# Talking-heads attention with a gated feed-forward layer: the score jobs run one slot further ahead

## The chip, the cores and the metric

The kernel runs on one core of a Trainium2 chip. The metric is the time of one execution on the device, in microseconds. The core has five engines that run in parallel, each through its own instructions in order: TensorE (PE in the profile; PEld is its weight load), VectorE (DVE), ScalarE (ACT), GpSimd (POOL) and SyncE (SP), which here issues nearly all DMA transfers. Engines wait for each other by semaphores. TensorE writes its results to PSUM, in banks that this program names; the other engines read them there.

## What is computed

```python
# q, k, v: 4 batches, 12 heads, 448 rows, head size 64
scores = q @ k.T / 8                                     # 448x448 for each head
scores = einsum('bhij,hg->bgij', scores, w_pre)          # mixes the 12 heads ("pre-mix")
e      = exp(scores - rowmax(scores))
attn   = e / (rowsum(e) + 1e-9)
attn   = einsum('bhij,hg->bgij', attn, w_post)           # mixes them again ("post-mix")
x      = attn @ v                                        # heads side by side: 1792 x 768
out    = (sigmoid(x @ w_gate) * (x @ w_val)) @ w_out     # 768 -> 1536 -> 768
```

## The kernel before

The program has two stages. Attention comes first and takes somewhat less than half of the span; the gated layer follows, and some of its preparations (weights turned into small pieces) run between the steps of attention.

**Blocks and units.** The 448 queries of a batch are cut into blocks of 120, 120, 120 and 88 queries, and a block into units of 20 queries, in each of which all 12 heads are held. A block has 6, 6, 6 or 5 units, a batch 23, all four 92. `first` holds the first unit of each block: 0, 6, 12, 18, 23, 29, 35, 41, 46, 52, 58, 64, 69 and so on. So unit 38 lies in the third block of batch 1, and unit 61 in the third block of batch 2.

**Score jobs.** For each block there are six jobs of `scores` (L155), one for each pair of heads, numbered c. A job is eight matmuls into two PSUM banks, and then two copies from them into `st` in SBUF (`keep`, L163): the even head's by ScalarE, the odd one's by VectorE. The banks are mostly the one pair `qk`, so the next job's matmuls wait until both copies of the last are done. In the fill, before the first unit, some jobs use the banks of other steps (`pm`, `mx`), which are free by then.

**A unit's way.** `regroup` (L199) is two DMA transfers, issued on SP, from `st` into one of four buffers `T`, in which the heads lie along the partitions. Then `premix` (L209, eight matmuls), `rowmax` into `nm` (VectorE), `expo` into `e` (two ScalarE instructions), norm and scale into `ph` (mostly GpSimd), `p_lo` into `pl` (VectorE), `postmix` (48 small matmuls into `mx`) and `mix` (ScalarE, out of PSUM). Once a whole block is mixed, `av` multiplies by V: six steps, two in every second slot of the block after, each pair evicted to `xt` by ScalarE and stored.

**Slots.** The order on every engine is written by hand, one slot for each unit and six ahead of the first (numbers -6 to -1, the fill). Slot s issues, in this order: on SP the regroup of unit s+6 (`LEAD` = 6) and the stores that are due; norm and scale of unit s+1; pre-mix and row maxima of unit s+3; the matmuls of the first score job planned for s; the first half of the exponentials of unit s+3, and after it the two copies of that job; `p_lo` of s+1; post-mix and mix of s; the second half of the exponentials; then what else is planned for the slot (loads of `k`, `q` and `v` on SP, the sums `v_abs` on ScalarE); then `av` and `moe.early`, the gated layer's preparations (loads into `raws` and a ScalarE step of line 1104); and last, if one is planned, a second score job. Each engine takes its own instructions in this order, and nothing but semaphores keeps the engines in the same slot.

**Where the score jobs stand.** `at(slot, function, ...)` plans a call, and `spread` divides a count evenly over slots. Before, the six jobs of block bi are spread from slot `first[bi-1] - 6` to slot `first[bi] - 6`, so the last of them stands one slot ahead of the block's first regroup. Where the block before has six units, that is a job in each slot. Where it has five, six jobs fall on five slots, and the first of these takes two. The `q` load of a block is planned four slots ahead of its first job. The six `k` loads of the next batch are spread over some slots in the middle of a batch, in the rest of the slot, behind its regroup. The first block's jobs run ahead of all slots (`ahead`).

Of the kernel before, what the change touches and what calls it, by code (L numbers as in the profile page):

```python
# [41 lines left out]
def _attention(ctx, tc, ins, B, H, S, D, xs, raws, make_moe):  # L42
# [4 lines left out]
    NP = H // 2  # L47
# [30 lines left out]
    def two_banks(pool, tag):  # L78
        return pool.tile([128, 2, 512], F32, tag=tag, name=tag)

    def qk_banks():
        return [ps_qk.tile([128, 512], F32, tag="qk", name="qk") for _ in range(2)]
# [47 lines left out]
    PB = NBK // B  # L130
    first = [blk[3] for blk in blocks] + [NU]
# [23 lines left out]
    def scores(bi, c, sc):  # L155
        b, n = blocks[bi][0], R * blocks[bi][4]
        q, k = q_t[bi], k_t[b, c]
        for s0, s1 in ((0, 64), (64, max(n, 100))):
            for e in range(2):
                rows = slice(64 * e, 64 * e + 64)  # L160
                nc.tensor.matmul(sc[e][s0:s1, :S], lhsT=q[c][rows, s0:s1], rhs=k[rows, :], start=True, stop=True)  # L161

    def keep(bi, c, e, sc):  # L163
        n = R * blocks[bi][4]
        if c == e == 0:
            st_t[bi] = stg[bi % ST].tile([QB, H, S], F32, tag="st", name="st")
        (nc.vector.tensor_copy if e else nc.scalar.copy)(st_t[bi][:n, 2 * c + e], sc[e][:n, :S])  # L167
# [41 lines left out]
    def premix(u):  # L209
        T = t_bufs[u % len(t_bufs)]  # L210
        banks = units[u][2]
        for x in range(2):
            for i, bank in enumerate(banks):
                rows = slice(64, 64 + HK) if i else slice(0, 64)
                nc.tensor.matmul(pm[bank][64 * x:64 * x + 64, :S], lhsT=w1[rows], rhs=T[rows, x], start=True, stop=True)  # L215

    def rowmax(u):
        nm = sm.tile([128, 2], F32, tag="nm", name="nm")
        for i, bank in enumerate(units[u][2]):
            nc.vector.tensor_reduce(nm[:, i:i + 1], pm[bank][:, :S], axis=AX.X, op=ALU.max, negate=True)  # L220
        nm_t[u] = nm

    def expo(u, i):
        if i == 0:
            e_t[u] = ep.tile([128, 2, S], F32, tag="e", name="e")
            ss_t[u] = sm.tile([128, 2], F32, tag="ss", name="ss")
        nc.scalar.activation(out=e_t[u][:, i], in_=pm[units[u][2][i]][:, :S], func=AF.Exp, bias=nm_t[u][:, i:i + 1],  # L227
                             scale=1.0, accum_out=ss_t[u][:, i:i + 1])

    def norm(u):  # L230
        ss = ss_t[u][:, :len(units[u][1])]
        (nc.vector if u >= NU - LAST else nc.gpsimd).tensor_scalar(ss, ss, 1e-9, 1.0 / P_UP, op0=ALU.add, op1=ALU.mult)
        nc.vector.reciprocal(ss, ss)  # L233

    def scale(u):

        ph = pp.tile([128, 2, S], F16, tag="ph", name="ph")
        for i in range(len(units[u][1])):
            e, ss = e_t[u][:, i], ss_t[u][:, i:i + 1]
            if u >= NU - LAST:  # L240
                nc.scalar.activation(out=ph[:, i], in_=e, func=AF.Copy, scale=ss)  # L241
            else:
                nc.gpsimd.tensor_scalar(ph[:, i], e, ss, 1.0, op0=ALU.mult, op1=ALU.mult)  # L243
        p_t[u] = [ph]

    def p_lo(u):
        pl = pp.tile([128, 2, S], F16, tag="pl", name="pl")
        for i in range(len(units[u][1])):
            nc.vector.scalar_tensor_tensor(pl[:, i], e_t[u][:, i], ss_t[u][:, i:i + 1], p_t[u][0][:, i],  # L249
                                           op0=ALU.mult, op1=ALU.subtract)  # L250
        p_t[u].append(pl)
# [14 lines left out]
    def mix(u):  # L266
        bi, r0s = units[u][:2]
        out = mixes[bi % 2].rearrange("p j h s -> p (j h) s")[:, :, r0s[0]:r0s[-1] + R]
        nc.scalar.activation(out=out.rearrange("p g (y r) -> p y g r", r=HALF), in_=mx_t.pop(u), func=AF.Copy,  # L269
                             scale=1.0 / (P_UP * W_UP))  # L270
# [4 lines left out]
    def flush():  # L275
        while stores:
            nc.sync.dma_start(out=stores[0][0], in_=stores.pop(0)[1])
# [31 lines left out]
    LEAD = 6  # L309
# [5 lines left out]
    def at(slot, fn, *args):  # L315
        plan.setdefault(slot, []).append((fn, args))

    def spread(i, n, s0, s1):
        return s0 + i * (s1 - s0) // n

    taken = {EARLY_AT[k] + slot for k in range(moe.EARLY) for slot in (11, 12)}
    for b in range(B):
        f = first[PB * b]
        for u in range(NQ):
            at(f + 2 + 2 * u, v_load, b, u)
        s = f + 5
        for i in range(H // 2):
            s = max(s + 1, f + 6 + 2 * (2 * i // QUAD))
            while s in taken:
                s += 1  # L330
            at(s, v_sum, b, i)
        if b % 2:
            at(s + 1, v_bound, b, 0)
        if b == 1:
            for step, slot in enumerate(BOUND[1:]):
                at(s + 1 + slot, v_bound, b, step + 1)
        for c in range(NP if b else 0):
            at(spread(c, NP, first[PB * (b - 1)] + 6, first[PB * b - 1] - LEAD - 2), k_load, b, c)
    for bi in range(1, NBK):
        s0, s1 = first[bi - 1] - LEAD, first[bi] - LEAD  # L340
        for c in range(NP):
            at(spread(c, NP, s0, s1), scores, bi, c)
        if bi > 1:
            at(s0 - 4, q_load, bi)
    for bi in range(NBK):
        s0 = first[bi + 1]
        s1 = first[bi + 2] if bi + 2 < len(first) else s0
# [58 lines left out]
    def rows_until(u, done):  # L406
        while done < min(NU, u + 1):
            regroup(done)
            done += 1
        return done  # L410

    next_dma = 0
    for s in range(min(min(plan), -LEAD), max(plan) + 1):
        next_dma = rows_until(s + LEAD, next_dma)
        flush()
        todo = plan.get(s, ())
        jobs = [args for fn, args in todo if fn is scores]
        ahead_u = [(s + SOFT, i) for i in range(len(units[s + SOFT][1]))] if 0 <= s + SOFT < NU else []
        if 0 <= s + 1 < NU:
            norm(s + 1)  # L420
            scale(s + 1)
        if ahead_u:
            premix(s + SOFT)
            rowmax(s + SOFT)

        def gated():
            for i in range(len(units[s][1])):
                moe.slot(units[s][3] + i)

        soon = NU - 7 <= s < NU  # L430
        if soon:
            for c in hooks.pop(s, ()):
                c.close()
            gated()

        def job(bi, c):
            if s == -LEAD:
                sc = pm[2:]
            elif s in (-4, -2):
                mx = two_banks(ps_mx, "mx")  # L440
                sc = [mx[:, e] for e in range(2)]
            else:
                sc = qk_banks()
            scores(bi, c, sc)
            return lambda e: keep(bi, c, e, sc)

        kept = job(*jobs[0]) if jobs else None
        for i, e in enumerate(ahead_u[:1]):
            expo(*e)
        if kept:  # L450
            kept(0)
            kept(1)
        for c in hooks.get(s, ()):
            c.close()
        if 0 <= s + 1 < NU:
            p_lo(s + 1)
        tail = (av, moe.between, moe.early)
        if s == NU - 1:
            nc.scalar.activation(out=iw, in_=sw, func=AF.Sigmoid)
        if 0 <= s < NU:  # L460
            postmix(s)
        elif s >= NU:
            moe.slot(NG + s - NU)
        if 0 <= s < NU:
            mix(s)
        for e in ahead_u[1:]:
            expo(*e)
        while late:
            late.pop(0)()
        for fn, args in todo:  # L470
            if fn is not scores and fn not in tail:
                fn(*args)
        if s >= NU - LEAD - 3:
            next_dma = rows_until(s + 1 + LEAD, next_dma)
        if 0 <= s < NU and not soon:
            gated()
        for fn, args in todo:
            if fn in tail:
                fn(*args)
        for args in jobs[1:]:  # L480
            kept = job(*args)
            kept(0)
            kept(1)
    return moe
# [21 lines left out]
class _Moe:  # L506
# [14 lines left out]
    NP = 7  # L521
# [797 lines left out]
```

## Time and profile before

| | |
|---|---|
| time, median of three runs | 787.21 us (787.09 to 788.61) |
| the profiled execution's own time | 788.01 us |
| its span in the trace | 786.2 us |
| granted TensorE clock, mean | 0.995 |
| TensorE busy | 761.5 us, 97% |
| VectorE busy | 630.9 us, 80% |
| ScalarE busy | 572.9 us, 73% |
| GpSimd busy | 250.5 us, 32% |

The trace is from one execution, another than the three timed ones. Its time is 1.8 us longer than the span between its first and last instruction. Busy shares are means over two stages that differ: in attention VectorE and ScalarE have far more to do than in the gated layer.

### The profile page before, as it was taken

What the parts mean: (1) busy time and instruction counts of PE and PEld (TensorE: products, weight loads), DVE (VectorE), ACT (ScalarE), POOL (GpSimd) and SP (SyncE); (2) the same over time, 40 slices, a digit from 0 to 9 for tenths busy, and PEclk for the clock granted to TensorE, in tenths of its full rate; (3) what the DMA queues carried; (4) which work ended last, traced back from release to release, by engine and by line L of the source; (5) the groups of instructions that cost most, each with busy time, mean ns of one, the idle gap of its engine ahead of it and who ended that gap; (6) DMA issues with size and microseconds to landing.
All of it is one profiled execution on the core that took longest, in us unless ns stands there. A gap on an engine that the chain in (4) does not pass through costs nothing.

```text
span 786.2 us, 23669 instructions
## 1 busy us (share of the span) xinstructions
PE 761.5 (97%) x9623; PEld 422.2 (54%) x9623; DVE 630.9 (80%) x1093; ACT 572.9 (73%) x1145; POOL 250.5 (32%) x418
## 2 busy tenths in 40 slices
PE   8899999899999999879999999999999999999998
PEld 2365666566556666554555555555555555555554
DVE  4988899799978998879997989588876999997111
ACT  4899999889999899886876866577756784563000
POOL 2564547354544455200312222224222221010000
PEclk9999999999999999989999999999999999999999
DMA  6786668758886574738507284664567788995001
GB/s 198 242 272 222 209 219 261 259 172 245 253 262 199 188 240 167 234 84 293 176 3 257 83 304 151 250 222 141 198 208 264 272 307 311 387 347 212 36 36 70
DMA packets 81118, 166.17 MB, mean 211 GB/s; under 512 B 20721, under 2 KB 58193, under 8 KB 81009
## 3 DMA queue, kind: packets, MB, share of 16 engines
q1 hardware_dynamic: 73006, 133.14, 51.5%
q0 software_dynamic: 7728, 31.27, 10.3%
q8 instruction: 75, 1.23, 0.7%
q14 instruction: 35, 0.28, 0.1%
q10 hardware_dynamic: 274, 0.25, 0.1%
HBM read 87.77 MB, written 38.15 MB: 160 GB/s over the span
## 4 chain that ended last, share of the span: by engine, by line
PE 84%; ACT 7%; DMA 3%; DVE 2%; issue 1%; SPq 1%; POOL 1%; DVEq 0%; ACTq 0%; POOLq 0%
PE bank L1173 34%; PE bank L1184 18%; PE pm L215 9%; PE av L290 8%; PE qk L161 7%; PE mx L261 7%; DMA T<-st 2%; ACT e L227 2%; ACT mix L269 2%; ACT m L1152 1%; DVE nm L220 1%; ACT st L167 1%; DVE m L1157 1%; PE pm L161 1%; SPq L205 1%
## 5 line engine op out<-in xcount | busy, mean ns | idle before, releaser
L1173 PEld LDWEIGHTS <-m 128*128 128x128 f16 x1512 | 147.7, 98 | 140.1 <-DVE m L1157 2.1
L1173 PE MATMUL bank<-m,m 128*128 128x448 f16 x1116 | 214.2, 352 | 1.7 <-DVE m L1157 1.7
L243 POOL TENSOR_SCALAR ph<-e,ss 128x448 f16<-128x448 f32 x173 | 108.0, 635 | 139.7 <-DVE ss L233 90.6
L227 ACT ACTIVATE e<-pm,nm 128x448 f32<-128x448 f32 x177 | 113.8, 643 | 28.2 <-DVE nm L220 25.3
L220 DVE TENSOR_REDUCE nm<-pm 128x1 f32<-128x448 f32 x177 | 101.6, 613 | 31.1 <-PE pm L215 25.9
L249 DVE SCALAR_TENSOR_TENSOR pl<-e,ss,ph 128x448 f16<-128x448 f32 x180 | 114.7, 677 | 0.7 <-ACT ph L241 0.7
L215 PE MATMUL pm<-T,w 64*64 64x448 f32 (+1 forms) x708 | 105.2, 560 | 7.4 <-DMA T<-st 3.6
L1184 PEld LDWEIGHTS <-m 128*128 128x128 f16 x756 | 74.0, 98 | 69.0
L269 ACT ACTIVATE mix<-mx 128x960 f32<-128x960 f32 (+1 forms) x92 | 104.6, 1137 | 2.7 <-PE mx L261 2.7
L261 PEld LDWEIGHTS <-ph 64*128 64x128 f16 x2880 | 63.8, 94 | 70.9 <-issue 44.3
L161 PE MATMUL qk<-k,q 64*64 64x448 f32 (+1 forms) x712 | 96.2, 539 | 1.0 <-ACT st L167 1.0
L1184 PE MATMUL bank<-m,m 128*128 128x448 f16 x468 | 92.9, 352 | 0.0
L290 PE MATMUL av<-mix,v 128*64 128x120 f32 (+1 forms) x1472 | 82.9, 266 | 0.6 <-ACT xt L298 0.6
L261 PE MATMUL mx<-w2hi,ph 64*128 64x60 f16 x1440 | 71.4, 189 | 7.2 <-ACT mix L269 6.8
L1173 PE MATMUL bank<-m 128*128 128x448 f16 x396 | 77.9, 352 | 0.0
L290 PEld LDWEIGHTS av<-mix,v 128*64 128x64 f32 x1472 | 72.8, 139 | 3.9 <-ACT xt L298 1.0
L1110 POOL CAST raws<-raws 128x768 f16<-128x768 bf16 x28 | 30.9, 1102 | 137.8 <-ACT raws L1104 137.8
L261 PE MATMUL mx<-w2hi,pl 64*128 64x60 f16 x1440 | 70.5, 188 | 1.1 <-issue 0.5
L261 PE MATMUL mx<-w2lo,ph 64*128 64x60 f16 x1440 | 70.5, 188 | 0.0
L1104 ACT ACTIVATE raws<-raws 128x768 int16<-128x768 int8 (+1 forms) x72 | 60.4, 839 | 10.8 <-POOL raws L1110 10.5
L1200 DVE TENSOR_TENSOR m<-bank,m 128x448 f32<-128x448 f32 x72 | 44.5, 620 | 23.6 <-PE bank L1173 15.3
L261 PEld LDWEIGHTS <-pl 64*128 64x128 f16 x1440 | 61.3, 93 | 1.1 <-DVE pl L249 1.1
(136 smaller groups left out, 1081.9 us busy)
## 6 DMA issues: line engine op xcount, KB each, us to landing
T<-st SPq DMA_DIRECT2D x175, 210.0 KB
m<-w SPq DMA_DIRECT2D x60, 384.0 KB
raws<-in_w_dram SPq DMA_DIRECT2D x28, 767.6 KB
hs<-m POOLq DMA_DIRECT2D x48, 224.0 KB, 3.4
m<-hs SPq DMA_DIRECT2D x15, 672.0 KB
w<-m POOLq DMA_DIRECT2D x21, 384.0 KB, 4.4
w<-raws POOLq DMA_DIRECT2D x20, 384.0 KB, 4.6
v<-in_vb_dram SPq DMA_DIRECT2D x12, 512.0 KB
```

The source lines that it names most:

```text
L161: nc.tensor.matmul(sc[e][s0:s1, :S], lhsT=q[c][rows, s0:s1], rhs=k[rows, :], start=True, stop=True)
L215: nc.tensor.matmul(pm[bank][64 * x:64 * x + 64, :S], lhsT=w1[rows], rhs=T[rows, x], start=True, stop=True)
L220: nc.vector.tensor_reduce(nm[:, i:i + 1], pm[bank][:, :S], axis=AX.X, op=ALU.max, negate=True)
L227: nc.scalar.activation(out=e_t[u][:, i], in_=pm[units[u][2][i]][:, :S], func=AF.Exp, bias=nm_t[u][:, i:i + 1], scale=1.0, accum_out=ss_t[u ...
L243: nc.gpsimd.tensor_scalar(ph[:, i], e, ss, 1.0, op0=ALU.mult, op1=ALU.mult)
L249: nc.vector.scalar_tensor_tensor(pl[:, i], e_t[u][:, i], ss_t[u][:, i:i + 1], p_t[u][0][:, i], op0=ALU.mult, op1=ALU.subtract)
L261: nc.tensor.matmul(mx[:, x, i, jb * HK:(jb + 1) * HK], lhsT=p[rows, i, JB[jb]:JB[jb] + 128], rhs=w[rows], start=(k == 0), stop=(k == 2))
L269: nc.scalar.activation(out=out.rearrange("p g (y r) -> p y g r", r=HALF), in_=mx_t.pop(u), func=AF.Copy, scale=1.0 / (P_UP * W_UP))
L290: nc.tensor.matmul(av_t[bi][64 * i:64 * i + 64, c % 2, :n], lhsT=vt[b, u][:, h + i, jb, :], rhs=mixes[bi % 2][:, jb, 2 * c + i, :n], start ...
L1104: self.nc.scalar.activation(out=out, in_=src, func=AF.Copy, scale=by)
L1173: self.nc.tensor.matmul(self.f32(bank), lhsT=w[a][:, k], rhs=x[b][:, k], start=self.START[i] and k == r == 0, stop=k == self.KH - 1 and r ...
L1184: self.nc.tensor.matmul(self.f32(bank), lhsT=w[a][:, k], rhs=b[bb], start=self.START[i] and j == k == r == 0, stop=j == OUT_TILES - 1 and ...
```

## The change

- The six score jobs of block bi are spread from slot `first[bi-1] - 7` to slot `first[bi] - 7`, one slot earlier than before. The jobs that would fall in slot -7, which does not exist, go into slot -6: there are two in that slot now.
- The `q` load of a block is planned relative to its first job, so it is one slot earlier too.
- The `k` loads of the next batch are spread over one slot more: the last of them come a slot later.
- In the fill, the jobs that use the `mx` banks are those of slots -5 and -3 instead of -4 and -2, and the second job of slot -6 takes the `qk` banks.

```diff
@@ -335,11 +335,11 @@
             for step, slot in enumerate(BOUND[1:]):
                 at(s + 1 + slot, v_bound, b, step + 1)
         for c in range(NP if b else 0):
-            at(spread(c, NP, first[PB * (b - 1)] + 6, first[PB * b - 1] - LEAD - 2), k_load, b, c)
+            at(spread(c, NP, first[PB * (b - 1)] + 6, first[PB * b - 1] - LEAD - 1), k_load, b, c)
     for bi in range(1, NBK):
-        s0, s1 = first[bi - 1] - LEAD, first[bi] - LEAD
+        s0, s1 = first[bi - 1] - LEAD - 1, first[bi] - LEAD - 1
         for c in range(NP):
-            at(spread(c, NP, s0, s1), scores, bi, c)
+            at(max(spread(c, NP, s0, s1), -LEAD), scores, bi, c)
         if bi > 1:
             at(s0 - 4, q_load, bi)
     for bi in range(NBK):
@@ -433,10 +433,10 @@
                 c.close()
             gated()
 
-        def job(bi, c):
-            if s == -LEAD:
+        def job(bi, c, more=False):
+            if s == -LEAD and not more:
                 sc = pm[2:]
-            elif s in (-4, -2):
+            elif s in (-5, -3):
                 mx = two_banks(ps_mx, "mx")
                 sc = [mx[:, e] for e in range(2)]
             else:
@@ -478,7 +478,7 @@
             if fn in tail:
                 fn(*args)
         for args in jobs[1:]:
-            kept = job(*args)
+            kept = job(*args, True)
             kept(0)
             kept(1)
     return moe
```

What it does to the order is shown at three places.

ScalarE at the end of slot 34 and in slot 35 (batch 1), before. `e` is half of an exponential, `st<-qk` the copy of a score job, `mix` and `xt` are evictions, `raws` is the early weight step.

```order
L227 ACTIVATE e,ss<-pm_117,nm 128x448
L180 ACTIVATE v_abs,vm<-v 128x512
L1104 ACTIVATE raws<-raws 128x384
L227 ACTIVATE e,ss<-pm_115,nm 128x448
L167 COPY st<-qk 120x448
L269 ACTIVATE mix_168<-mx 128x4x48x5
L227 ACTIVATE e,ss<-pm_116,nm 128x448
L180 ACTIVATE v_abs,vm<-v 128x512
L298 ACTIVATE xt<-av,sw 128x240
L167 COPY st<-qk 120x448
```

The same place in the changed kernel:

```order
L227 ACTIVATE e,ss<-pm_117,nm 128x448
L180 ACTIVATE v_abs,vm<-v 128x512
L1104 ACTIVATE raws<-raws 128x384
L167 COPY st<-qk 120x448
L227 ACTIVATE e,ss<-pm_115,nm 128x448
L167 COPY st<-qk 120x448
L269 ACTIVATE mix_168<-mx 128x4x48x5
L227 ACTIVATE e,ss<-pm_116,nm 128x448
L180 ACTIVATE v_abs,vm<-v 128x512
L298 ACTIVATE xt<-av,sw 128x240
```

The copy of the second job has moved from the end of slot 35, behind `xt`, to the end of slot 34, behind `raws`. The same happens at slots 11 and 12 and, without the row of `raws`, at slots 57 and 58.

SP from the regroup of unit 37 (`T_171`) to that of unit 39 (`T_173`), before; each row of `T` is the two transfers of one unit.

```order
L205 DMA T_171<-st 120x1x448 x2
L138 DMA k<-in_kp_dram 128x448 x2
L148 DMA q<-in_qp_dram 128x720
L1063 DMA raws<-in_w_dram 128x1533
L205 DMA T_172<-st 120x1x448 x2
L277 DMA xs<-xt 128x2x120
L138 DMA k<-in_kp_dram 128x448
L205 DMA T_173<-st 120x1x448 x2
```

The same place in the changed kernel, from the `k` load ahead of unit 37's regroup on:

```order
L138 DMA k<-in_kp_dram 128x448
L148 DMA q<-in_qp_dram 128x720
L1063 DMA raws<-in_w_dram 128x1536
L205 DMA T_171<-st 120x1x448 x2
L138 DMA k<-in_kp_dram 128x448
L1063 DMA raws<-in_w_dram 128x1533
L205 DMA T_172<-st 120x1x448 x2
L277 DMA xs<-xt 128x2x120
L138 DMA k<-in_kp_dram 128x448
L205 DMA T_173<-st 120x1x448 x2
```

The `q` load of 128x720 stands ahead of unit 37's regroup instead of ahead of unit 38's (`T_172`), and one of the two `k` loads between units 37 and 38 is gone from there; it comes later.

SP in the fill, from the regroup of unit 1 (`T_171`) to that of unit 4 (`T_170`), before:

```order
L205 DMA T_171<-st 120x1x448 x2
L205 DMA T_172<-st 120x1x448 x2
L148 DMA q<-in_qp_dram 128x720
L205 DMA T_173<-st 120x1x448 x2
L205 DMA T_170<-st 120x1x448 x2
```

and in the changed kernel:

```order
L205 DMA T_171<-st 120x1x448 x2
L148 DMA q<-in_qp_dram 128x720
L205 DMA T_172<-st 120x1x448 x2
L205 DMA T_173<-st 120x1x448 x2
L205 DMA T_170<-st 120x1x448 x2
```

The `q` load of query block 2 stands ahead of unit 2's regroup (`T_172`) instead of behind it.

## Rows read from the trace of the kernel before

**Rows 1.** The page, part 1: span, then busy time, share and instructions.

```profile
span 786.2 us, 23669 instructions
...
PE 761.5 (97%) x9623; PEld 422.2 (54%) x9623; DVE 630.9 (80%) x1093; ACT 572.9 (73%) x1145; POOL 250.5 (32%) x418
```

**Rows 2.** Waits of TensorE: us in total, times, longest us.

```profile
PE mx L261 <- ACT mix L269: 6.8, 3, 5.1
PE pm L215 <- DMA T<-st: 3.6, 2, 2.0
...
PE qk L161 <- ACT st L167: 1.0, 1, 1.0
```

**Rows 3.** Chain of work, 116 to 152: start us, us, what.

```profile
137.14 6.64 DMA T<-st
...
145.69 0.75 PE qk L161 x6
146.44 0.77 PE mx L261 x48
147.21 1.79 PE av L290 x32
149.00 0.91 PE qk L161 x6
```

**Rows 4.** Chain of work, 200 to 236.

```profile
218.61 7.73 DMA T<-st
...
228.28 0.75 PE qk L161 x6
```

**Rows 5.** Windows: us, busy (count) of PE, PEld, DVE, ACT, POOL; clock, DMA.

```profile
132.00:144.00 12.00, 9.99 (x234) 6.13 (x231) 9.89 (x21) 12.00 (x30) 7.69 (x12) 1.00 0.84 271
212.00:228.00 16.00, 14.44 (x328) 8.97 (x322) 12.91 (x28) 15.91 (x40) 9.83 (x15) 1.00 0.85 264
```

**Rows 6.** Chain of work, 290 to 366 (slot 80).

```profile
305.68 0.42 ACT st L167
...
307.18 0.84 PE mx L261 x48
```

**Rows 7.** Timeline, ScalarE, 140.9 to 147.2: start, us, [idle before <-releaser].

```profile
141.47 0.68 ACT L227 ACTIVATE e<-pm,nm 128x448 f32<-128x448 f32 x1
...
144.68 0.63 ACT L1104 ACTIVATE raws<-raws 128x384 int16<-128x384 int8 x1
146.44 0.63 ACT L227 ACTIVATE e<-pm,nm 128x448 f32<-128x448 f32 x1 [1.12 <-DVE nm L220]
```

**Rows 8.** DMA, 130 to 146: mean rate, and issues with KB each.

```profile
DMA packets 2749, 4.24 MB, mean 265 GB/s; under 512 B 726, under 2 KB 2554, under 8 KB 2746
...
k<-in_kp_dram SPq DMA_DIRECT2D x4, 224.0 KB
...
q<-in_qp_dram SPq DMA_DIRECT2D x1, 360.0 KB
```

**Rows 9.** Timeline of ScalarE, 224.8 to 229.5.

```profile
225.50 0.55 ACT L167 COPY st<-qk 90x448 f32<-90x448 f32 x1
...
228.03 0.23 ACT L180 ACTIVATION_READ_ACCUMULATOR v_abs<-v 128x1 f32 x1
```

**Rows 10.** Chain of work, 58 to 76.

```profile
68.19 0.98 PE qk L161 x6
...
69.93 0.91 PE pm L215 x8
```

**Rows 11.** Timeline of ScalarE, 60 to 70.

```profile
61.09 0.55 ACT L167 COPY st<-qk 90x448 f32<-90x448 f32 x1
...
63.70 0.60 ACT L1104 ACTIVATE raws<-raws 128x384 int16<-128x384 int8 x1
```

**Rows 12.** Chain of work, 0 to 62.

```profile
14.83 4.86 DMA T<-st
```

**Rows 13.** Timeline of VectorE, 20 to 27.

```profile
25.05 0.62 DVE L220 TENSOR_REDUCE nm<-pm 128x1 f32<-128x448 f32 x1 [1.37 <-PE av L215]
```

## The prediction

> **What bounds the kernel now.** I read the page first: TensorE is busy for 761.5 us of a span of 786.2 us [rows 1], so all its idle time together is about 25 us, and a change that takes no TensorE work away can win only where TensorE now waits. Next the waits of TensorE [rows 2]. The largest entry, 6.8 us behind `mix`, lies after slot 80, where no score job stands before or after; the change leaves it alone. The entry that the change can reach is the pre-mix that waits for the regroup transfer into `T`: 3.6 us in two places.
>
> Then the chain of work, to see those two places. The first is unit 38 (slot 35): its transfer is issued at 137.14 and lands 6.64 us later, at 143.78; the slot's score job follows at 145.69 [rows 3]. The second is unit 61 (slot 58): issued at 218.61, landed at 226.34, score job at 228.28 [rows 4]. Both stand in the slot where a batch's last query block has only five units, so that six score jobs fall on five slots and one slot takes two: slots 12, 35 and 58 now.
>
> Last, the window view around both [rows 5]: from 132 to 144 us ScalarE is busy for 12.00 of 12.00 us, from 212 to 228 for 15.91 of 16.00. So while TensorE waits for `T`, ScalarE has no slack at all. I rest the forecast on this: the stall has two causes, one behind the other, and the change loosens only the first.
>
> **The change part by part.** It adds and removes no instruction. Each score job goes one slot earlier, with its matmuls (0.75 us on TensorE in slot 35 [rows 3]) and its two copies (0.42 us on ScalarE [rows 6]). In the long run each slot still has one job; what differs is five places.
>
> *The doubled slot, batch 1.* Slots 34 and 35 change roles: slot 34 now has two jobs, slot 35 one. The second job stands at the end of its slot. On TensorE it comes after the post-mix of slot 34, in time that is now the stall, and costs nothing there; it is gone from behind the attention-times-V matmuls of slot 35, where it took 0.91 us of the chain (0.75 for the eight matmuls alone) [rows 3]. But both jobs share the two `qk` banks, so the job of slot 35 must wait for ScalarE's copy of the second job of slot 34, and that copy stands on ScalarE behind `v_abs` and the early weight step of line 1104. That step starts at 144.68 and takes 0.63 us [rows 7]; with 0.42 for the copy the banks come free at 145.73. The job of slot 35 starts at 145.69 now, so it is not earlier, however early `T` lands. What is won is the removed job: 0.75 us. Bounds: if ScalarE were no obstacle, the win would be this 0.75 plus the earlier landing. One `k` load of 224 KB has moved from ahead of unit 38's transfer to behind it; at the mean of 265 GB/s [rows 8] that is 0.85 us, 1.6 us in all. If the queue's other move (third rival) makes ScalarE 0.8 us later, nothing is won: 0.1 us lost. I take -0.75, since ScalarE's row is the nearer one.
>
> *The doubled slot, batch 2.* The same at slots 57 and 58. The copy of slot 57's first job ends at 226.05 (225.50 + 0.55), and the read-out of `v_abs` at 228.26 (228.03 + 0.23) [rows 9]. The second job starts at 226.05 on TensorE, 0.75, then the pre-mix of unit 61, 0.91 [rows 10], to 227.7; the copy that frees the banks ends at 228.26 + 0.42 = 228.68, so slot 58's job starts 0.4 us later than now (228.28 [rows 4]), and its slot lacks 0.75 of work: -0.35. Bounds -1.6 and +0.5, found as above.
>
> *The doubled slot, batch 0.* Slots 11 and 12. There is no stall for `T` here to fill, and ScalarE is again the late one. The copy of slot 11's job ends at 61.64 (61.09 + 0.55), so the second job runs to 62.4 and the pre-mix of unit 15 to 63.3; the early step ends at 64.30 (63.70 + 0.60) and the copy behind it at 64.72 [rows 11]. TensorE waits for it for 1.4 us, then does job 0.75, post-mix 0.77, attention times V 1.79 [rows 3], pre-mix 0.91: 68.94 at the job of slot 13. Now that job starts at 68.19, itself after a wait [rows 10]. So +0.75; some of it is caught up on ScalarE in slot 14, and I take +0.6. Bounds: -1.0, if TensorE's one wait for `st` there (1.0 us [rows 2]) goes and none takes its place; +1.4, the whole new wait.
>
> *The fill.* Slot -6 takes two jobs. The second uses the `qk` banks, and all jobs keep their banks in turn, so the fill's PSUM order is as before; the extra job moves ahead of the first pre-mix, where TensorE is idle while the first `T` lands: nothing. The load of query block 2 moves from behind unit 2's transfer to ahead of it on SP. That transfer's second half is issued at 14.83 and lands 4.86 us later [rows 12]; 360 KB at 265 GB/s [rows 8] puts 1.36 us ahead of it. VectorE is idle for 1.37 us before unit 3's row maxima [rows 13], which hides just that. I take +0.25, between 0 (hidden) and +1.25 (if the load takes twice its share, with two transfers in flight beside it).
>
> *The end.* Slot 80 loses the last job, which is what the extra one in slot -6 pays for. There ScalarE leads the chain: `st` 0.42 at 305.68, then `mix`, then TensorE at 307.18 [rows 6]. -0.42; bounds 0 (VectorE's copy or the post-mix is next by then) and -0.75 (the matmuls).
>
> *The rest at nothing.* The first regroup of a block no longer waits on SP for the copies of the slot before. It frees SP by one to two microseconds, but `T` of those units lands well ahead of need, except around units 38 and 61, which are costed above. `q` loads elsewhere move past one regroup; the cover is the four `T` buffers, and it fails only where the DMA engines are full (third rival). After 363 us TensorE runs without a wait that the change touches, so the gated stage just starts as much earlier or later as attention ends.
>
> **The sum.** -0.75 - 0.35 + 0.6 + 0.25 - 0.42 = -0.67 us. The profiled execution took 788.01 us, 1.8 us of it around the span; it lies 0.8 us above the median of the three runs (787.21). 788.01 - 0.67 - 0.8 = **786.5 us**. Times of this kernel differ by 0.2% (1.6 us) before a measurement can tell them from no change, and this gain is smaller.
>
> **The rivals.**
>
> *Both stalls paid back (faster).* `T` is what TensorE waits for, and ScalarE's backlog goes with the stall because its work is pulled forward as well. Then each place gives 0.85 + 0.75 = 1.6, the end 0.42, batch 0 and the fill nothing: -3.6 us, 783.6; with batch 0's present wait gone as well 782.6. For it: the waits of TensorE name the transfer in both places, and ScalarE is idle for 1.12 us after its own backlog, at 146.44 [rows 7]. Against it: 12.00 of 12.00 us before that [rows 5]. [...]
>
> *The query load makes the units before late (slower).* The load of 360 KB moves from ahead of units 38 and 61 to ahead of units 37 and 60 too, where it adds 1.36 us. It decides from the point where unit 37's row maxima come after 141.47, when ScalarE now takes up its exponential [rows 7]. If they come 0.8 us later, ScalarE's whole slot 34 does, the copy that frees the banks with it, and batches 1 and 2 turn to +0.1 and +0.5; the same load costs the fill its 1.25. With batch 0 at +0.6 and the end at -0.42: +2.0 us, 789.2. For it: the DMA engines are at 84 and 85% in these windows [rows 5]. Against it: `T` of unit 37 made nobody wait.
>
> *The change doesn't do what it says.* If the transfers around units 38 and 61 land as late as now, because they queue in the DMA engines and not on SP, batches 1 and 2 come out the same as forecast, as their bound is ScalarE's copy. So this case has no time of its own and lies within the first.
>
> **How the numbers follow.** Forecast 0.5, both stalls paid back 0.25, query load 0.2, something I do not see 0.05. The forecast's own spread, from its bounds, is 785.2 to 788.0. The range takes in most of the rivals: **783.2 to 789.2**. Faster by over 0.2% (under 785.6): 0.25 for the second case and a little of the first, 0.30. Slower (over 788.8): 0.2 and a little, 0.21. Within: 0.49.
>
> **What would show it.** Right: no wait for `T` is left in slots 35 and 58, but the score matmuls of slots 12, 35 and 58 wait for ScalarE's `st` copy, about 1.4 us at slot 12 and 1 us at the others; ScalarE stays full from 132 to 145 us; the last wait for `st` in slot 80 is gone. The second case: in slots 35 and 58 TensorE has no idle time, and attention ends 3 us or more earlier. The third: pre-mixes of units 37 and 60 wait for `T`. I would be wrong altogether if the waits behind `mix` after 330 us (5.1 us in one place) change by more than a microsecond, since I price that stretch as moved whole.

## The result, and the profile after

The changed kernel takes 791.65 us (median of 7 runs, 790.32 to 794.61), the kernel before 787.09 us in the same seven rounds. The ratio is 1.0058, with a 95% interval of 1.0041 to 1.0075: slower by 0.58%, some 4.6 us. The forecast was 786.5, its range ended at 789.2. The profiled execution of the changed kernel took 792.47 us, with a span of 790.7 us.

The page after, part 1, and the waits of TensorE in that execution (us in total, times, longest):

```profile
span 790.7 us, 23684 instructions
...
PE 764.2 (97%) x9623; PEld 422.1 (53%) x9623; DVE 631.1 (80%) x1093; ACT 573.5 (73%) x1145; POOL 250.8 (32%) x418
```

```profile
PE mx L261 <- ACT mix L269: 6.3, 2, 5.1
PE qk L161 <- ACT st L167: 3.3, 6, 1.4
PE mx L261 <- issue: 2.8, 2, 1.8
PE pm L215 <- DMA T<-st: 2.1, 2, 1.8
...
PE av L290 <- issue: 1.2, 1, 1.2
```

Against [rows 2], the waits for `T` have left slots 35 and 58 (the two that stand here, 1.8 and 0.3 us, lie in the fill, before units 2 and 0), waits for ScalarE's copy `st` have come in six places, and the third wait for `mix`, the one of slot 80, is gone, all as the prediction said. (For slot 80 it spoke of the wait for `st`: TensorE waits there for `mix`, which stands on ScalarE behind the copy `st`.) In slot 35 the wait is for the copy that it named. The timeline of ScalarE in the changed kernel:

```profile
144.03 0.63 ACT L227 ACTIVATE e<-pm,nm 128x448 f32<-128x448 f32 x1 [0.47 <-DVE nm L220]
...
147.26 0.56 ACT L1104 ACTIVATE raws<-raws 128x384 int16<-128x384 int8 x1
147.71 0.54 ACT L167 COPY st<-qk 120x448 f32<-120x448 f32 x1
```

and of TensorE at the same place:

```profile
146.99 0.96 PE L161 MATMUL qk<-k,q 64*64 64x448 f32 x2
148.30 0.97 PE L161 MATMUL qk<-k,q 64*64 64x448 f32 x6 [0.35 <-ACT st L167]
```

The copy behind the early step of line 1104 ends at 148.25, and the job of slot 35 goes on at 148.30. By the profile's idle time the jobs of slots 12 and 35 wait for it only 0.33 and 0.35 us. But in both, two of the eight matmuls start early and the other six 1.29 and 1.31 us after them (64.32 and 65.61 in slot 12), which is not far from the 1.4 and 1 us foretold: the two that have started count as busy meanwhile. The waits of 0.52, 0.43 and 1.42 us are those of the second jobs, in slots 11, 34 and 57, for the copy of the first; the job of slot 58 itself has none that the profile names, though its eight matmuls take 1.83 us.

One sign that I had named failed: ScalarE is not full. The slots of [rows 5] stand some 2 us later here; in the windows moved by as much (ScalarE is the fourth busy time) it has 11.30 of 12 and 14.24 of 16 us. The DMA share is 0.89 and 0.85 there, after 0.84 and 0.85.

```profile
134.10:146.10 12.00, 11.48 (x244) 6.64 (x244) 8.85 (x19) 11.30 (x29) 6.03 (x11) 1.00 0.89 271
...
214.00:230.00 16.00, 13.08 (x316) 8.23 (x308) 12.61 (x27) 14.24 (x36) 8.53 (x13) 1.00 0.85 262
```

What has grown are waits called "issue", in which TensorE waits for nothing that the profile names: 0.95 us at 129.90, 1.19 at 210.43 and 1.83 at 217.66, against 0.53 and 0.60 before. With them alone one would explain 2.8 of the 4.5 us between the two spans. That was my first reading, and the experiments bear it out only in part.

### The profile page after: what moved, and what is told of

Its sections match the earlier page's. It is cut to its first block, busy times and chain, and to the rows that moved or that the text cites. A ratio compares the mean times of both kernels' runs of the same rounds, so it can differ in the third digit from the quotient of the medians.

```text
span 790.7 us, 23684 instructions
## 1 busy us (share of the span) xinstructions
PE 764.2 (97%) x9623; PEld 422.1 (53%) x9623; DVE 631.1 (80%) x1093; ACT 573.5 (73%) x1145; POOL 250.8 (32%) x418
## 3 DMA queue, kind: packets, MB, share of 16 engines
q8 instruction: 75, 1.23, 0.7%
## 4 chain that ended last, share of the span: by engine, by line
PE 83%; ACT 8%; DMA 3%; DVE 3%; issue 2%; POOL 1%; SPq 0%; ACTq 0%; DVEq 0%; POOLq 0%
PE bank L1173 34%; PE bank L1184 18%; PE pm L215 9%; PE av L290 8%; PE qk L161 7%; PE mx L261 7%; ACT mix L269 2%; ACT e L227 2%; ACT m L1152 1%; DMA k<-in_kp_dram 1%; DMA T<-st 1%; ACT st L167 1%; DVE nm L220 1%; ACT v_abs L180 1%; DVE pl L249 1%
## 5 line engine op out<-in xcount | busy, mean ns | idle before, releaser
L161 PE MATMUL qk<-k,q 64*64 64x448 f32 (+1 forms) x712 | 98.1, 540 | 5.0 <-ACT st L167 3.3
```

## The experiments

Each kernel was timed in 12 executions unless said, beside 23 to 35 of the kernel before on the same chip. Single executions of one program differ by several us there (the kernel before: 783.8 to 794.7 us), so a ratio has an interval of about 0.2% to each side.

**Jobs or loads.** The jobs alone are the change with these lines as before:

```diff
-            at(spread(c, NP, first[PB * (b - 1)] + 6, first[PB * b - 1] - LEAD - 1), k_load, b, c)
+            at(spread(c, NP, first[PB * (b - 1)] + 6, first[PB * b - 1] - LEAD - 2), k_load, b, c)
-            at(s0 - 4, q_load, bi)
+            at(s0 - 3, q_load, bi)
```

Expected: "

> The score jobs stand one slot earlier as in the change, but the q and k loads stand in the slots of the kernel before. Theory A (TensorE waits for its own code, which is loaded by DMA and comes late where the moved q and k loads crowd the DMA engines; in the changed kernel's trace these waits, named issue, are 0.95, 1.19 and 1.83 us, against 0.53 and 0.60 before): most of that goes away, what stays is the doubled slot at 11/12 (+1.0 in the trace) and the fill, so about 788.0 to 788.8 us and issue waits under 1.5 us in all. Theory B (the jobs' own order costs the 4.6 us, the loads do not matter): 791.2 to 792. Theory C (the q load ahead of the transfer into T costs it): T of unit 37 and of unit 2 are on time again, 789.5 to 790.5.

"

Measured 791.62 us, ratio 1.0060 (1.0034 to 1.0086). The loads alone are the kernel before with `- LEAD - 1` in the k loads and `s0 - 5` in the q load. Expected: "

> The q loads stand one slot earlier and the k loads are spread over one slot more, as in the change, but the score jobs stand where they stood before. Theory A (code loads crowded out by the moved loads): issue waits of 2 us or more in all and 789 to 790.5 us. Theory B (the order of the jobs): 787.1 us, as before. Theory C (T late behind the q load): waits for T in the slots before the doubled ones, 788.2 to 789.2 us.

"

Measured 787.75 us, ratio 1.0010 (0.9982 to 1.0039). So the loads by themselves cost nothing that can be measured, and with the jobs alone the whole loss is there. But the first kernel does not show that loads are harmless beside moved jobs. There the jobs catch up with their `q`; TensorE's waits in it:

```profile
PE qk L161 <- DMA q<-in_qp_dram: 3.5, 2, 1.8
```

Either the `q` load goes ahead of the transfers into `T`, or the job waits for it: two ways to pay for the same slot.

**The borders of the code.** The issue waits have a pattern. I counted all TensorE instructions of a trace in their order, waits and registers included. In the kernel before, the issue waits of 0.53 and 0.60 us stand at numbers 4545 and 8641; in the changed kernel at 5057, 8641 and 8897. All leave 193 when divided by 256. Each ended 1.35 to 1.6 us after the end of one transfer of the queue named instruction, 16 KB each. The DMA view of the changed kernel from 214.9 to 216.3 us has one of them (packets, MB, share of the engines), among engines that the kernel's own loads fill:

```profile
q1 hardware_dynamic: 239, 0.37, 81.9%
q8 instruction: 1, 0.02, 4.6%
```

and the chain from 205 to 220 us shows the wait for it, in the middle of a post-mix:

```profile
215.12 0.71 PE mx L261 x44
215.83 1.83 issue
217.66 0.23 PE mx L261 x4
```

I read these as waits for TensorE's own code, which would come in pieces of 256 instructions during the run, now and then a piece late. The page of either kernel has 75 transfers of 16 KB on that queue (1.23 MB), about one for each 256 of the 19,348 TensorE instructions counted in the trace of before (19,354 in that of the change); with 66 instructions more, as below, the page of either has 76. No trace names the engine that such a transfer is for.

To move the borders and as little else as possible, I wrote the warm-up matmuls at the start in smaller pieces, which adds 66 instructions (`warm(7)` and `warm(4)` as below), in the changed kernel and in the one before:

```diff
-    warm(7)
+    warm(28, 128)
-    warm(4)
+    warm(16, 128)
```

Expected of the changed kernel: "

> The changed kernel, with the 11 warm-up matmuls of 512 columns written as 44 of 128 columns: as much streaming, but 66 more TensorE instructions ahead of everything, so that each block of code begins 66 instructions earlier in the work; nothing else moves. Theory A: the issue waits (at 129.90, 210.43 and 217.66) stand at other instructions and have other sizes, and the time moves by more than 0.8 us, most likely down to 789 to 791. Theories B and C: 791.7, within 0.5.

" Of the kernel before: "

> The kernel before with the same 66 instructions ahead. Theory A: its two issue waits (0.53 at 117.09 and 0.60 at 208.77) go or others come, the time moves by up to 1.5 us either way, 786 to 788.5. Theories B and C: 787.1, within 0.4.

"

Measured: 788.89 us, ratio 1.0018 (0.9995 to 1.0041), for the change; 788.63 us, 1.0008 (0.9981 to 1.0035), for before. The issue waits of the changed kernel did move: those at 129.90, 210.43 and 217.66 have no counterpart, and at the borders at 54.03 and 60.54 TensorE stands 0.59 and 0.54 us. Then the kernel before with `warm(15, 240)` for `warm(7)`, which gives its code the 16 instructions by which a moved job shifts it: "

> The kernel before with 8 more TensorE instruction pairs at the start (7 warm-up matmuls of 512 columns written as 15 of 240): the code blocks stand against the work where they stand in the changed kernel, and no job is moved. Theory E: slower like the change, 790 to 792 us, with issue waits of 3 us or more. Theory D: as before, within 0.8 us.

"

Measured 787.99 us, 1.0001 (0.9983 to 1.0020): that shift by itself costs nothing that can be measured. Two more kernels at the end of the study come back to this.

**The doubled slot.** The changed kernel with the second, not the first, of five slots taking two jobs, so that slots 12, 35 and 58 are doubled as before:

```diff
-            at(max(spread(c, NP, s0, s1), -LEAD), scores, bi, c)
+            at(max(s0 + c - (c > 1) if s1 - s0 < NP else s0 + c, -LEAD), scores, bi, c)
```

Expected: "

> The changed kernel, but where six jobs fall on five slots the second of these slots takes two, not the first: the doubled slots are 12, 35 and 58 again, as before the change, while every other job stands one slot earlier. Theory D (the doubled slot in front of a long attention-times-V slot is what costs: the stretch that ScalarE bounds ends a slot earlier, and the next slot's work of TensorE lies bare; the traces with moved jobs all lose 1 to 2.3 us over slots 11 to 13 and those with unmoved jobs nothing): the loss there is gone, 788 to 789.5 us, 0.0 to 0.25% above before. Theory E (TensorE's code blocks, which begin 16 instructions earlier in the work wherever a job has come ahead, meet the busy DMA queues at a worse place): the time stays at 790.5 to 792.

" And beside it the changed kernel once more: "

> The changed kernel once more, unchanged, on the same chip as the three others and with a second trace. Theory D: again a loss of about 1 us over slots 11 to 13 against the trace of before, while issue waits stand elsewhere. Theory E: issue waits at the same instructions as in its first trace (129.90, 210.43 and 217.66) and of similar size. Both: 790.5 to 792.5 us.

"

Measured: 788.74 us, 1.0020 (0.9998 to 1.0042), against 792.56 us, 1.0059 (1.0037 to 1.0081), for the unchanged repeat. With the doubled slot put back, about two thirds of the loss are gone. The repeat's chain shows two of the three code waits of the first trace again, at the very same instructions (after 29 and after 44 matmuls) and of other sizes; the one of 129.90 is missing:

```profile
208.41 1.68 PE av L290 x29
210.09 0.50 issue
...
215.27 0.71 PE mx L261 x44
215.99 1.56 issue
```

The third place for the doubled slot, in the kernel before (`s0 + c - (c > 2)` where six jobs fall on five slots): "

> The kernel before, with the doubled slot two slots later in each of the three places: 14, 37 and 60 instead of 12, 35 and 58, where the sums v_abs are over or nearly so. Theory D: the wait for ScalarE's copy behind the doubled slot (0.96 us at 68.19 in the trace of before, about 1.1 at 149) shrinks, 785 to 786.8 us. Theory E: within 1 us of before either way, as code blocks move by 16 instructions over two slots only.

"

Measured 787.83 us, 1.0004 (0.9980 to 1.0028): no gain, where theory D had foretold one.

The doubled slot moved alone, in the kernel before (slots 11, 34 and 57):

```diff
-            at(spread(c, NP, s0, s1), scores, bi, c)
+            at(s0 - (s1 - s0 < NP) + c, scores, bi, c)
```

Expected: "

> The kernel before, with one thing of the change alone: the second job of the doubled slots 12, 35 and 58 stands one slot earlier, at the end of slots 11, 34 and 57; no other job and no load moves, the fill is as before. Theory D (the doubled slot is the cost): slower by 2 to 4 us, 789.5 to 791.5. Rival F (the fill, with its two jobs in slot -6 and the banks taken in another order, and the rest of the shift carry it): within 1 us of before.

" and for a repeat: "

> The kernel before with the doubled slot alone moved to 11, 34 and 57, a second time. If the doubled slot is the cause, 1.5 to 3 us over before again and, pooled with the first 12 executions (+1.4 us), clear of none; if the first was chance, within 0.7 us of before.

"

Measured 788.46 us, 1.0018 (1.0000 to 1.0036), and 787.61 us, 1.0010 (0.9995 to 1.0025). That is 1.4 and 0.8 us by the medians' ratios, not 2 to 4, though the first interval reaches 2.8: theory D falls in the size that I gave it. A repeat of the kernel with the doubled slot put back, "

> The changed kernel with the doubled slots back at 12, 35 and 58, a second time. If the doubled slot is the cause of nearly all, 787.5 to 789 us; if something else in the shift costs 1.5 us or more, 789 to 790.5 again.

", gave 788.91 us, 1.0016 (0.9993 to 1.0038), as the first time.

**The second job ahead of the early work**, so that its copy stands ahead of line 1104 and `xt` on ScalarE:

```diff
+        for args in jobs[1:]:
+            kept = job(*args, True)
+            kept(0)
+            kept(1)
         for fn, args in todo:
             if fn in tail:
                 fn(*args)
-        for args in jobs[1:]:
...
```

Expected in the changed kernel: "

> The changed kernel, but a second job of a slot stands ahead of the attention-times-V steps and the gated layer's early work of its slot, not behind them; so ScalarE's copy that frees the two qk banks stands ahead of the early step of line 1104 and of the eviction xt. Theory D in my own form (the next slot's job waits for that copy): 788 to 789.5 us, the waits for st in slots 12, 35 and 58 gone. If the doubled slot costs because ScalarE and VectorE are full there whatever their order, it stays at 790.5 to 792.5.

" and the same edit in the kernel before: "

> The same edit on the kernel before: the second job of slots 12, 35 and 58 ahead of that slot's attention-times-V and early steps. Theory D in my own form: the waits for st of about 1 us (68.19 in the trace of before, 149 in those of its variants) go, 785 to 786.8 us. Otherwise within 1 us of before.

"

Measured 789.99 us (9 executions), 1.0033 (1.0017 to 1.0048), and 788.89 us, 1.0017 (1.0003 to 1.0031). In the changed kernel it gains some 2 us (1.0033 against 1.0058, with intervals that still touch); in the kernel before it costs 1.3 us, where I had expected a gain or nothing. The longest wait for `st` falls from 1.4 to 0.5 us, and what TensorE waits for now is the transfer into `T`:

```profile
PE pm L215 <- DMA T<-st: 3.3, 5, 1.1
...
PE qk L161 <- ACT st L167: 1.6, 4, 0.5
```

**The kernel before once more**, for a second trace: "

> The kernel before once more, for a second trace of the very same program. If the waits for T on which the forecast rests (2.01 us in slot 35, 1.56 us in slot 58) belong to the kernel, they stand there again within 0.5 us; if they belong to one execution, as traces of its near variants suggest, one or both are missing, and the stretch from the pre-mix of unit 36 to that of unit 41 takes 20.4 to 21.3 us in place of 21.88. The time: as before, within 0.5 us.

"

Measured 788.60 us, 1.0010 (0.9989 to 1.0031): this is what no change at all looks like. The pre-mix of unit 38, which waited 2.01 us for `T` in the first trace, in the timeline of the second:

```profile
145.36 1.35 PE L215 MATMUL pm<-T,w 64*64 64x448 f32 x6 [0.29 <-DMA T<-st]
```

The wait on which the largest term of the forecast rested is 0.29 us here. The wait of unit 61 stands there again, with 1.1 us.

**The fill.** The kernel before with only block 1's jobs moved (`spread(c, NP, s0, s1) - (bi == 1)`, not below slot -6, and the change's banks): "

> The kernel before, with only the fill as in the change: the six jobs of query block 1 stand one slot earlier (two in slot -6, none in slot -1), with the change's PSUM banks; all later jobs and all loads are as before. If the fill carries what the doubled slot does not (about 1.5 us), 788.7 to 790 us; if it carries nothing, as before within 0.8 us.

" The changed kernel with only block 1's jobs and banks as before: "

> The changed kernel with the fill as before: query block 1's jobs in slots -6 to -1, one each, all later jobs one slot earlier as in the change, so that slot -1 has two. If the fill costs 1.5 us, 789.5 to 790.5 us; if the doubled slots carry all, 791 to 792.5.

"

Measured 788.19 us, 1.0011 (0.9988 to 1.0033), and 793.09 us (6 executions), 1.0071 (1.0046 to 1.0097). So the fill's jobs show no cost of their own, and putting them back brings nothing back.

**The borders again.** The changed kernel with 66 more instructions, a second time: "

> The changed kernel with 66 more TensorE instructions at the start, a second time. If the place of the code blocks in the work carries more than half of the loss, 788.5 to 790 us again and, pooled with the first 12 executions, clearly under the change's 791.6 to 792.6; if the first was chance, 791 to 793.

" And with 32 more (`warm(17, 208)`, `warm(10, 208)`): "

> The changed kernel with 32 more TensorE instructions at the start (the 11 warm-up matmuls of 512 columns written as 27 of 208), so that the code blocks begin at yet other places in the work. If the change's own place is an unlucky one among many, 788 to 790 us; if the code blocks do not matter, 791 to 793. Either way the stretch from the pre-mix of unit 14 to that of unit 20 takes 23.0 to 23.6 us, as the doubled slot 11 is kept.

"

Measured 789.19 us, 1.0008 (0.9979 to 1.0037), and 791.31 us, 1.0038 (1.0013 to 1.0064). The first is no chance then: by these ratios the same order of work, with its code cut at other places, loses a third or less of what the change loses; cut at a third place, about two thirds. In the trace of the repeat there is not one issue wait, and its span is the shortest of all:

```profile
span 783.6 us, 23750 instructions
```

No kernel tried beats the one before.

**The granted clock.** A rival that the record settles is TensorE's clock. All 20 traces have a fall of the granted clock from 1.00 to 0.50 at the end of attention (334.7 to 341.5 us in the first of before). In five of them it falls earlier too, for 3.4 us at a time, six falls in all. Each of the six begins between 0.3 us before and 1.3 us after the end of a wait of TensorE of 1.65 to 2.7 us. Not every such wait is followed by a fall: the 2.01 us of the first trace of before are not. The second trace of before has a code wait of 1.66 us that ends at 41.71, and then (the clock is the third number from the end):

```profile
41.71 0.20 PE L261 MATMUL mx<-w2hi,ph 64*128 64x60 f16 x2 [1.66 <-issue]
```

```profile
40.00:43.00 3.00, 1.34 (x55) 0.98 (x53) 2.42 (x6) 1.73 (x6) 2.12 (x4) 1.00 0.67 218
43.00:46.40 3.40, 3.40 (x63) 1.50 (x54) 2.35 (x5) 2.45 (x6) 1.02 (x3) 0.50 0.88 251
```

The traces with such falls are those with a mean clock of 0.994 or less. Of the kernel before, beside these experiments, the 87 of 154 executions at 0.995 or more took 787.0 us in the mean, the 60 at 0.993 or 0.994 took 788.3. Of the change, the 11 of 19 at 0.995 or more took 791.7. So the falls are part of the scatter, and at an equal clock the change still loses 4.7 us. At 0.995 or more, over all chips, the doubled slot put back takes 788.1 us, the change with 66 more instructions 788.6, with 32 more 790.1, and the doubled slot alone 787.9: much the same picture as the ratios give.

**What the traces say together.** The table has stretches between the first matmuls of two pre-mixes, in us, read in the timeline of each trace, and the sum of code waits up to the gated stage (the time between the starts of the two instructions at a border, less 0.05 us, counted where it exceeds 0.3 us and ends 1.2 to 1.8 us after an instruction transfer of 16 KB; in the first trace of the change that holds at four of 58 borders, and the other 54 have 0.12 us or less; the smallest of those counted can be ordinary waits). The traces of four variants are left out (third place, job ahead in both kernels, fill moved).

| kernel | units 14 to 20 | 36 to 41 | 57 to 64 | 83 to 91 | code waits |
|---|---|---|---|---|---|
| before, and again | 22.24, 22.20 | 21.88, 20.55 | 27.99, 30.35 | 25.68, 25.67 | 1.75, 3.62 |
| before: loads alone, 66 and 16 more instructions | 22.22, 23.60, 22.24 | 20.38, 20.38, 21.26 | 29.60, 28.86, 32.39 | 25.66, 25.67, 25.68 | 2.69, 5.07, 2.78 |
| doubled slot alone, and again | 23.42, 23.15 | 21.30, 21.15 | 29.16, 30.22 | 25.67, 25.69 | 2.30, 3.06 |
| change, and again | 23.22, 23.26 | 21.74, 23.06 | 30.00, 29.70 | 25.24, 25.25 | 4.89, 2.68 |
| jobs alone; fill as before | 23.59, 23.15 | 24.22, 22.99 | 29.20, 30.93 | 25.24, 25.25 | 5.12, 6.13 |
| change, 66 more instructions, and again; 32 more | 23.97, 23.15, 23.35 | 21.31, 21.32, 21.81 | 28.52, 28.26, 30.31 | 25.25, 25.24, 25.25 | 2.06, 0.00, 4.95 |
| doubled slot put back, and again | 23.02, 22.22 | 21.81, 21.11 | 29.50, 27.52 | 25.25, 25.25 | 0.42, 2.31 |

## Why the prediction was wrong

The step that failed is "The doubled slot, batch 1", with its -0.75 us, and beneath it the place where the sum began: a stall that comes in some executions and not in others was taken for one of the kernel. The runs show 1 to 1.5 us lost there. Beside it, one effect was put at nothing without a reason: jobs that move also move the borders of TensorE's code. Point by point:

- **Batch 1.** In the five traces with jobs and doubled slot as before, the stretch from unit 36 to 41 takes 20.9 us in the mean, in the seven with the moved jobs and slot 34 doubled 22.35: +1.5 us in place of -0.75. Three of the twelve hold something else: code waits of 2.1 and 2.4 us (16 more instructions, 21.26; fill as before, 22.99) and a fall of the clock (jobs alone, 24.22). Without them the means are 20.8 and 21.85, +1.05. The first trace of before (21.88) is the worst of its group, as it has the 2.01 us for `T`, which its repeat lacks; the kernel with only the fill moved has 1.71 us there, and the other three traces of the group none over 0.25. Where it is missing, there was nothing to win. What the change adds is two waits in a row. The first is the third rival's: unit 37's pre-mix waits for its `T`, behind the earlier `q` load. In the repeat of the change, the timelines of TensorE and ScalarE:

```profile
142.65 0.59 PE L215 MATMUL pm<-T,w 64*64 64x448 f32 x2 [0.84 <-DMA T<-st]
```

```profile
144.37 0.64 ACT L227 ACTIVATE e<-pm,nm 128x448 f32<-128x448 f32 x1 [1.63 <-DVE nm L220]
...
148.05 0.53 ACT L167 COPY st<-qk 120x448 f32<-120x448 f32 x1
```

  ScalarE takes up unit 37's exponential 8.54 us after the pre-mix of unit 36 began (135.83), where [rows 7] has it 6.8 us after (141.47, the pre-mix at 134.69). Then the copy that frees the banks comes at the end of that late slot, as I had said. I had given the late `T` a chance of 0.2 and the point from which it decides; in the repeat it was passed by 1.8 us. In the first trace of the change the same delay is smaller: the profile names no wait, but the eight matmuls of unit 37's pre-mix start over 1.50 us (141.25 to 142.75) in place of 0.45 in the first trace of before, and ScalarE takes up the exponential 7.2 us after unit 36's pre-mix. That it is the `q` load beside the moved jobs which makes `T` late there is an inference. In the eleven traces in which `q` loads or jobs stand as before, these eight matmuls start within 0.45 us; in six of the nine with both moved they take 0.85 to 2.53 us, in the other three 0.45. It was not isolated further.
- **Batch 0, +0.6.** Right in sign and near in size: all nine traces with slot 11 doubled have 23.15 to 23.97 us from unit 14 to 20, those with slot 12 doubled in the kernel before 22.20 to 22.24, but for one with a code wait of 1.21 us in it (23.60). That is some +0.95. (With the slot put back one trace has 22.22, the other 23.02; why is open.) The chain of the changed kernel shows the step as it was worked out: the copy behind the early step, then job, post-mix, attention times V and pre-mix bare behind it.

```profile
64.71 0.43 ACT raws L1104
65.14 0.43 ACT st L167
65.57 0.04 issue
65.61 0.97 PE qk L161 x5
66.58 0.77 PE mx L261 x48
67.35 1.79 PE av L290 x32
69.14 0.91 PE pm L215 x8
```

- **Batch 2, -0.35.** Not to be told: the stretch from unit 57 to 64 varies by over 4 us between traces of one order (27.99 to 32.39).
- **The fill, +0.25.** In the time its jobs alone are not to be told from none (1.0011). In both traces of the change unit 2's pre-mix waits for its `T`, which now stands behind the load of query block 2, for 1.77 and 1.66 us, and unit 6's begins at 32.51 and 32.38 us, against 31.64 and 31.82 in the two traces of before. That is 0.6 to 0.9 us, more than I took and within the bounds; but the loads alone have 31.11, so the place of the load by itself is not shown to cost it. (By its own terms the upper bound is 2 x 1.36 - 1.37 = 1.35, not 1.25.)
- **The end, -0.42.** Right to the digit: 25.24 to 25.25 us from unit 83 to 91 in all nine traces of the table with moved jobs, 25.66 to 25.69 in all seven without. It and batch 0 are the two terms that depend on no transfer, and the two that came out near.
- **The code waits** were in the trace of before, as "issue", 0.53 and 0.60 us, and I left them out. They average 4.7 us in the four traces of the change and its two near variants (jobs alone, fill as before), 3.2 in the five of the kernel before and its near variants, and come to 0.0 to 4.95 with the change's borders moved. So part of the loss, about 1.5 us by these means, may lie in the change's borders; with a spread of 2.7 to 6.1 us within the four, the share is not firm.

These pieces, 1.05 + 0.95 - 0.43 + 1.5, make some 3 of the 4.6 us, without the fill. What stays open is how they act together. Putting the doubled slot back and moving the code borders by 66 instructions each bring back 3 to 4 us; the doubled slot alone, moved in the kernel before, costs some 1 us (1.0018 and 1.0010), and 66 instructions more there change nothing that can be measured. The parts do not add up as independent terms would, and which wait of one place sets off which of the next was not settled. So it is shown that the loss comes with the moved jobs, and that most of it goes when either the doubled slots are put back or the borders of the code are moved by 66 instructions; the full path to 4.6 us is not shown.

## What to carry to other kernels

Before a forecast rests on a stall of 1 or 2 us in a stretch full of transfers, take a second trace of the same program: here one of two such stalls was all but absent in the next trace. Work that is pulled ahead needs its inputs ahead as well: ask which transfers that someone waits for then stand behind them. Here, in a stretch with a DMA share of 0.84 in the first trace of before and of 0.89 in that of the change, unit 37's pre-mix waited 0.84 us for its `T` behind the earlier `q` load in the repeat of the change, and nothing that the profile names in the first trace. Ask of each added place which engine must free its banks, and what lies bare behind it once that engine is done. And before a loss of half a percent is put down to an order of work, move the borders of the code in both kernels and time them again: here the same order took 3 us less.

## What the runs showed of the hardware

The pages have 75 transfers of 16 KB on the queue named instruction, beside the 19,246 matmuls and weight loads of TensorE, and give their time as 0.7% of the same 16 DMA engines of which they give the data's time as a share. I take them for TensorE's code. In the first trace of the change the starts of the two instructions at a border lie 0.49 to 2.02 us apart at four of the 58 borders up to 372 us, and 0.12 us or less at the others. The longest of these waits, 1.83 us by the profile's idle time, stands in the middle of a post-mix (48 matmuls with their weight loads in 0.77 us), and around the transfer ahead of it the kernel's own loads had 81.9% of the engines' time. The longest of all traces is 2.2 us (fill as before, in attention times V). The waits of TensorE have both under "issue". Sixty-six instructions more at the start took some 3 us from the time of the changed kernel (1.0018 and 1.0008 in place of 1.0058), and changed that of the kernel before by nothing that could be measured (1.0008).

A wait of TensorE of 1.65 us or more was in six cases followed by 3.4 us at a granted clock of 0.50 in place of 1.00 (43.00 to 46.40 in the second trace of before), and in others, as the 2.01 us at 143.92 in the first trace of before, by none.
